# First two batches of a linear-attention and MLP-mixer kernel: casts and features dealt out anew, denominators ahead of kv, w_ch2 and one store issued elsewhere

## The chip, the cores and the metric

The kernel runs on one core of one Trainium2 chip. The metric is device time in microseconds (us), the median of several executions. Shorter names stand for the engines, as in the profile: PE is TensorE (matmuls), PEld its weight loads, DVE is VectorE, ACT is ScalarE, POOL is GpSimd, SP is SyncE, which here only issues transfers. A DMA is a transfer between HBM and the on-chip memory, or a transposing copy within it.

## The reference

Two layers, for 8 batches of 576 rows (`seq`), 8 heads of 64:

```python
def _attn_ref(q, k, v):                       # (8, 8, 576, 64) each
    def phi(x, c, s):                         # c = cos, s = sin of pi/2 * pos / 576
        r = np.maximum(x, 0.0)
        return np.concatenate([r * c, r * s], axis=-1)
    q_p, k_p = phi(q, cos_w, sin_w), phi(k, cos_w, sin_w)
    kv = np.einsum('bhsf,bhsd->bhfd', k_p, v)
    z = np.sum(k_p, axis=2)
    num = np.einsum('bhsf,bhfd->bhsd', q_p, kv)
    den = np.einsum('bhsf,bhf->bhs', q_p, z)[..., None] + 1e-06
    return num / den

def _moe_ref(x, w_tok1, w_tok2, w_ch1, w_ch2):  # x: (8, 576, 512), heads side by side
    h = np.maximum(x.transpose(0, 2, 1) @ w_tok1, 0.0) @ w_tok2      # 576 -> 256 -> 576
    u = x + h.transpose(0, 2, 1)
    h2 = np.maximum(u @ w_ch1, 0.0) @ w_ch2                          # 512 -> 1536 -> 512
    return u + h2
```

Inputs and output are float32; the kernel multiplies in bf16 and sums in float32.

## The kernel before, in words

**Tiling.** A batch's 576 rows are 4 chunks of 128 (row p*4+r is in chunk r) and a tail of 64 rows; the tails of two batches share one 128-row tile. So a batch has five chunks, 0 to 3 and R (the tail). `feature` (lines 274-291) makes the cos half (j = 0) or the sin half (j = 1) of q's or k's features for one chunk, on VectorE, or on ScalarE where `on_act` is set. `values` casts v to bf16 beside a column of ones. `ksum` and `ksum_out` sum the k features (z), `dens` and `dens_out` make the reciprocal of the denominator, `kv` and `kv_out` make kv and copy it out of PSUM, `q_trans` turns q's features so that TensorE can contract over them (`q_trans_beside` the tail's), `num_half` and `num` make the numerators and divide. `tok1`, `tok2`, `turned_*`, `c_main`, `o_mix` and `o_step` are the mixer: its first layer over tokens, the second, u transposed, the channel layer up and the channel layer down.

**Staging.** The first batch has a front of its own, `first_front` (lines 717 to 820). It works in halves of four heads (g = 0, 1), since its inputs come in halves. TensorE also runs `busy` matmuls on zeros there (tile `idle_ps`), whose results nobody reads. Behind it each batch's channel phase is a list of steps (`Channel.steps`): for batch 0 the steps 0 to 11 are `c_main` (the first three are done in the front), 12 and 13 are `o_mix`, and from 14 on each step is two matmuls of `o_step`. The attention of the next batches is woven into those steps: `pieces` gives a plan of (slot, function, arguments), and what stands at slot i is issued right after step i, in the order of the list. For batch 1 the plan is written out by hand: KS makes k's features of a chunk (with True the sin half is made by ScalarE), V casts values, KV is kv, QS makes q's features, QT turns them through TensorE and a ScalarE copy, N is numerators and division, O is 12.

**Order.** The scheduler is manual: every engine runs its own instructions in the order in which the code issues them. One call often issues on several engines (N: eight matmuls on TensorE, then an addition, a reciprocal and a multiplication on VectorE), and what stands behind a waiting instruction on its engine waits too. PSUM has 4 buffers of tag "mm" and 2 of tag "at" (the latter for kv of both halves, for `num_ps` and, in the second batch, for `idle_ps`); a new tile takes a buffer when the last reader of an older tile is done.

**Transfers.** SP issues most loads, all transposing copies of later batches and most stores, each in program order. GpSimd issues the three thirds of w_ch2 (`load_w_ch2`, line 208), converting to bf16, and batch 0's stores of chunks 2 and 3 (line 661). q and k of batch 2 are loaded only when the second third of w_ch2 has landed. GpSimd also casts w_tok1, w_tok2 and w_ch1 (lines 220 to 235).

Of the kernel before, what the change touches and what calls it, by code (L numbers as in the profile page):

```python
# [9 lines left out]
F32 = mybir.dt.float32  # L10
# [6 lines left out]
def kernel(  # L17
# [15 lines left out]
    nc = tc.nc  # L33
# [6 lines left out]
    P = 128  # L40
    R = S // P
# [174 lines left out]
    def busy(dst, times):  # L216
        for _i in range(times):
            nc.tensor.matmul(dst, ident, zeros[:, 0:dst.shape[-1]], start=True, stop=True)  # L218
# [19 lines left out]
    class Front:  # L238
# [81 lines left out]
        def dens(self, g):  # L320
            d_ps = ps_mm.tile([P, NSC * HH], F32, name="d_ps", tag="mm")
            for ci in range(NSC):
                for j in range(HH):
                    nc.tensor.matmul(d_ps[:, ci * HH + j:ci * HH + j + 1],
                                     self.qT_of(ci, g * HH + j), self.ks_sb[g][:, j:j + 1],
                                     start=True, stop=True)
            self.d_ps = d_ps
# [186 lines left out]
        def pieces(self, b, before):  # L514
# [7 lines left out]
            if first:  # L522
# [3 lines left out]
                def fill(times):  # L526
                    if not idle:
# [4 lines left out]
                plan = [(6, KS, 0), (6, KS, 1), (8, KS, 2, True), (9, KS, 3, True), (9, KS, R),  # L532
                        (10, before.tok2, R, None, False), (11, V, 0, act), (11, V, 2, pool),
                        (11, load_w_ch2, 0), (11, V, 3, pool), (11, load_w_ch2, 1),
                        (11, load_w_ch2, 2), (11, V, R, nc.vector), (11, V, 1, act)]
                plan += [(O + 1, KV, ci) for ci in range(NSC)]
                plan += [(O + 1, self.kv_out, (0, 1), (0, 1)), (O + 1, self.q_trans_beside),
                         (O + 1, QS, 0), (O + 1, fill, 2), (O + 1, QT, 0),
                         (O + 1, QS, 1), (O + 1, fill, 1), (O + 1, QT, 1),
                         (O + 1, QS, 2), (O + 1, fill, 1), (O + 1, QT, 2), (O + 1, N, R),  # L540
                         (O + 1, QS, 3, True), (O + 1, N, 0), (O + 2, N, 1), (O + 3, QT, 3),
                         (O + 5, N, 2), (O + 6, N, 3), (O + 8, before.tail_cast)]
# [52 lines left out]
    class Channel:  # L595
# [46 lines left out]
        def o_step(self, ci, lo, hi, cols=slice(0, Dm)):  # L642
# [16 lines left out]
            if ci < R:  # L659

                eng = nc.gpsimd if b == 0 and ci > 1 else nc.sync
                eng.dma_start(
                    out=out[b, 0:SM, cols].rearrange("(p r) d -> p r d", r=R)[:, ci, :], in_=o_sb)
                return
# [52 lines left out]
    def first_front(f):  # L717
# [13 lines left out]
        for ci in range(R):  # L731
            f.feature("k", ci, 0, heads[0])
            f.feature("k", ci, 1, heads[0])
            busy(idle_ps, 2)
            f.ksum(ci, 0)
            f.values(ci, nc.scalar, heads[0])
        f.k_side(R)
# [5 lines left out]
        for ci in range(R):  # L743
            f.feature("k", ci, 0, heads[1])
            if ci < 3:
                f.feature("k", ci, 1, heads[1])
        for ci in range(NSC):
            f.kv(ci, (0,))
        f.kv_out((0,))
        f.feature("k", 3, 1, heads[1], on_act=True)  # L750
        busy(idle_ps, 1)
        f.dens(0)
        f.dens_out(0)
        for ci in ORDER[:2]:
            f.num_half(ci, 0)
        f.values(3, nc.vector, heads[1])
        for ci in range(NSC):
            f.ksum(ci, 1)
        f.values(0, nc.scalar, heads[1])
        f.ksum_out(1)  # L760
        for ci in (1, 2):
            f.values(ci, nc.scalar, heads[1])
# [7 lines left out]
        for i in range(2):  # L770
            f.num_half(ORDER[i + 2], 0)
            f.tok1_half(ORDER[i], 0)
# [4 lines left out]
        f.dens(1)  # L777
        f.dens_out(1)
        permute_tok2(0, nc.scalar.copy)
        for ci in ORDER[:2]:  # L780
            f.num_half(ci, 1)
        for ci in ORDER[2:]:
            f.tok1_half(ci, 0)
# [136 lines left out]
```

## Time and profile before

| | |
|---|---|
| median of 3 executions | 271.11 us (271.05 to 271.15) |
| the profiled execution | 271.65 us |
| its span, first to last instruction | 269.8 us |
| TensorE busy in the span | 261.2 us (97%), 2041 matmuls |
| VectorE, ScalarE, GpSimd busy | 159.9, 127.6, 16.6 us |
| granted TensorE clock | 1.00 |
| the first batch's front (to the first h1T of line 613) | 0 to 26 us |
| the second batch's attention, from its kv to its first mixing matmul | 35.4 to 45.1 us |

A row of the timeline gives start, duration (from the first start to the last end, where rows are merged), engine, line, operation, the tiles written and read, the shape, and in brackets how long the engine sat idle before it and what released it. PE's duration of a matmul is longer than its share of the engine, because matmuls overlap: the distance between starts is what a row of them costs (0.216 us for 512 columns, 0.055 for 128, 0.029 for 65, 0.025 for 1).

### The profile page before, as it was taken

To read this page: it belongs to the slowest core of one execution; us is meant where nothing else is said; L and a number is where in the kernel's file an instruction comes from. 1 tells how busy PE (TensorE), PEld (TensorE's weight loads), DVE (VectorE), ACT (ScalarE), POOL (GpSimd) and SP (SyncE) were. 2 spreads that over 40 slices of the span, in tenths; PEclk is the share of its full clock that TensorE was granted. 3 is DMA by queue.
4 is the path that set the end of the run, shared out by engine and by line. 5 is a ranking of instruction groups with operands and counts; after the bars stand their busy time and mean duration, and the time that the engine had idled before them with its cause. 6 is when DMAs were issued, how large, how long until landed. Compare 5 with 4: busy or idle time off the path is not lost.

```text
span 269.8 us, 5150 instructions
## 1 busy us (share of the span) xinstructions
PE 261.2 (97%) x2041; PEld 140.5 (52%) x2062; DVE 159.9 (59%) x379; ACT 127.6 (47%) x231; POOL 16.6 (6%) x38
## 2 busy tenths in 40 slices
PE   7999988999999999999999999999999999999994
PEld 2685464456644455446644455446644455445543
DVE  5972558766467657677466757777466747720022
ACT  4774874508606173347616272446606372526400
POOL 2068130010000000000000000000000000000000
PEclk9999999999999999999999999999999999999999
DMA  7999999689999899679996999479974570170032
GB/s 232 366 391 378 332 137 230 235 225 242 182 298 300 238 232 286 199 148 247 168 300 101 278 262 302 131 171 260 222 266 117 156 119 0 47 209 0 2 104 91
DMA packets 92263, 55.32 MB, mean 205 GB/s; under 512 B 59472, under 2 KB 85968, under 8 KB 92240
## 3 DMA queue, kind: packets, MB, share of 16 engines
q1 hardware_dynamic: 89968, 52.38, 73.6%
q0 software_dynamic: 1744, 2.10, 4.4%
q10 hardware_dynamic: 528, 0.52, 0.6%
q8 instruction: 16, 0.26, 0.4%
q14 instruction: 7, 0.06, 0.1%
HBM read 35.85 MB, written 9.44 MB: 168 GB/s over the span
## 4 chain that ended last, share of the span: by engine, by line
PE 88%; DVE 5%; DMA 3%; issue 1%; ACT 1%; SPq 0%; POOL 0%; POOLq 0%; DVEq 0%
PE o_ps L649 33%; PE c_ps L609 25%; PE u_ps L460 6%; PE b_ps L436 6%; PE idle_ps L218 4%; PE ct_ps L629 3%; PE kv_ps L371 3%; DVE x_sb L426 2%; PE num_ps L419 2%; DMA qtt<-in_q_dram 2%; PE qT_ps L391 1%; DMA qpT_tail<-qp_tail 1%; PE c_ps L619 1%; PE b_ps L353 1%; DVE den L424 1%
## 5 line engine op out<-in xcount | busy, mean ns | idle before, releaser
L649 PE MATMUL o_ps<-w_ch,h1T 128*128 128x512 bf16 (+1 forms) x381 | 93.0, 372 | 0.6
L609 PE MATMUL c_ps<-uT,w_ch 128*128 128x512 bf16 (+2 forms) x384 | 91.2, 372 | 0.1
L613 ACT ACTIVATE h1T<-c_ps 128x512 bf16<-128x512 f32 x93 | 55.4, 598 | 61.3 <-PE c_ps L609 61.0
L649 PEld LDWEIGHTS <-h1T 128*128 128x128 bf16 x396 | 37.3, 98 | 39.6 <-issue 0.2
L609 PEld LDWEIGHTS <-w_ch 128*128 128x128 bf16 x384 | 33.5, 97 | 29.8
L658 DVE TENSOR_TENSOR o_sb<-o_ps,u_sb 128x512 f32<-128x512 f32 (+1 forms) x29 | 19.5, 672 | 27.3 <-PE o_ps L649 25.3
L467 ACT CAST u_bf<-u_sb 128x512 bf16<-128x512 f32 x28 | 17.3, 618 | 17.4 <-DVE u_sb L463 15.6
L460 PE MATMUL u_ps<-B,w_tok 128*128 128x512 bf16 x71 | 20.2, 379 | 0.2
L441 ACT ACTIVATE B<-b_ps 128x512 bf16<-128x512 f32 x7 | 4.2, 597 | 33.2 <-PE b_ps L436 33.2
L463 DVE TENSOR_TENSOR u_sb<-u_ps,x_sb 128x512 f32<-128x512 f32 x24 | 16.5, 690 | 5.6 <-PE u_ps L460 5.6
L629 PEld LDWEIGHTS <-w_ch 128*128 128x128 bf16 x192 | 13.9, 98 | 8.7
L290 DVE TENSOR_SCALAR kp<-kt,cos_t 128x512 bf16<-128x512 f32 (+1 forms) x36 | 16.1, 450 | 3.9 <-DMA kt<-in_k_dram 3.9
L290 DVE TENSOR_SCALAR qp<-qt,cos_t 128x512 bf16<-128x512 f32 (+1 forms) x35 | 16.2, 462 | 2.0 <-DMA qt<-in_q_dram 1.9
L426 DVE TENSOR_TENSOR x_sb<-num_ps,den 128x512 bf16<-128x512 f32 x24 | 16.6, 691 | 0.8
L629 PE MATMUL ct_ps<-uT_tail,w_ch 128*128 128x128 bf16 x192 | 16.9, 219 | 0.0
L301 ACT CAST v_aug<-vt 128x512 bf16<-128x512 f32 (+1 forms) x31 | 16.6, 576 | 0.1
L290 DVE TENSOR_SCALAR qp<-qt,sin_t 128x512 bf16<-128x512 f32 (+1 forms) x34 | 15.4, 453 | 0.0
L290 DVE TENSOR_SCALAR kp<-kt,sin_t 128x512 bf16<-128x512 f32 (+1 forms) x33 | 14.9, 452 | 0.0
L658 DVE TENSOR_TENSOR o_sb<-o_ps,u_tail 128x512 f32<-128x512 f32 x4 | 2.8, 691 | 19.0 <-PE o_ps L649 19.0
L218 PE MATMUL idle_ps<-zeros,ident 128*128 128x512 bf16 x33 | 12.0, 469 | 1.6 <-POOL ident masks.py:199 1.4
L436 PE MATMUL b_ps<-x_sb,w_tok 128*128 128x512 bf16 x48 | 13.3, 379 | 0.0
L419 PEld LDWEIGHTS <-qpT 128*128 128x128 bf16 x224 | 10.1, 98 | 5.5 <-ACT qpT L395 1.5
(112 smaller groups left out, 241.9 us busy)
## 6 DMA issues: line engine op xcount, KB each, us to landing
out_dram<-o_sb SPq DMA_DIRECT2D x29, 256.0 KB, 2.9
kt<-in_k_dram SPq DMA_DIRECT2D x7, 1024.0 KB, 6.8
vt<-in_v_dram SPq DMA_DIRECT2D x7, 1024.0 KB, 6.9
qt<-in_q_dram SPq DMA_DIRECT2D x7, 1024.0 KB, 8.6
w_stage<-in_moe_w_ch_dram SPq DMA_DIRECT2D x3, 512.0 KB, 9.3
w_ch<-in_moe_w_ch_dram POOLq DMA_DIRECT2D x3, 512.0 KB, 8.6
out_dram<-o_sb SPq DMA_DIRECT2D x10, 128.0 KB, 2.3
kt<-in_k_dram SPq DMA_DIRECT2D x2, 512.0 KB, 5.7
```

The source lines that it names most:

```text
L218: nc.tensor.matmul(dst, ident, zeros[:, 0:dst.shape[-1]], start=True, stop=True)
L290: nc.vector.tensor_scalar(o_ap, i_ap, scalar1=w, scalar2=0.0, op0=ALU.mult, op1=ALU.max)
L301: nc.scalar.copy(dst, src)
L426: nc.vector.tensor_mul(self.x_of(ci)[rows].rearrange("p (g j d) -> p g j d", g=2, j=HH), nv[:, :, :, 0:D], den.to_broadcast([rows.stop - r ...
L436: nc.tensor.matmul(self.b1_ps[mi], w, self.x_of(ci), start=(ci == ORDER[0]), stop=(ci == ORDER[-1]))
L460: nc.tensor.matmul(u_ps, w_tok2[:, ki, ci * P:(ci + 1) * P], self.B1[:, ki, :], start=(ki == 0), stop=(ki == NT - 1))
L467: nc.scalar.copy(self.ub[:, ci, :], u)
L609: nc.tensor.matmul(c_ps[:, lo:hi], w_ch1[:, ki, mi * P:(mi + 1) * P], uT[:, lo // P:hi // P, ki, :], start=(ki == 0), stop=(ki == NCC - 1))
L613: nc.scalar.activation(self.h1T[:, mi, :], c_ps, AF.Relu)
L629: nc.tensor.matmul(self.ct_ps[:, mi % R, :], w_ch1[:, ki, mi * P:(mi + 1) * P], self.tail.uT[:, ki, :], start=(mi % R == 0 and ki == 0), s ...
L649: nc.tensor.matmul(o_ps, h, w_ch2[:, ki, cols], start=(ki == 0 and b > 0), stop=(ki == NCH - 1))
L658: nc.vector.tensor_add(o_sb, o_ps, u)
```

## The change

Only the first two batches' attention and a few transfers are touched; the operations stay the same but for filler matmuls, and each is at another place or on another engine.

In the first batch's front: the sin features of k for chunks 2 and 3, second half of heads, are made by ScalarE ahead of `ksum_out(0)` (before: chunk 2's by VectorE, chunk 3's by ScalarE behind `kv_out`). The denominators of half 0 come ahead of kv of that half, the tail's four apart and behind it, and one filler is gone. The casts of values stand one by one between other ScalarE work. The first numerators come behind the sums of half 1, and the denominators of half 1 ahead of its kv.

In the second batch's plan: k's features of chunks 2 and 3 come at slots 6 and 7 (before 8 and 9). The casts of values come at slot 10, three by VectorE, one by GpSimd, one by ScalarE (before slot 11: two by ScalarE, two by GpSimd, one by VectorE). The first third of w_ch2 is issued on GpSimd ahead of its cast of values, the others right behind it. `before.tok2(R)` is a slot later. Four fillers stand before kv. kv's copies are shared by ScalarE (half 0) and VectorE (half 1), where ScalarE did both. The tail's numerators come ahead of q's features of chunk 2, and the turning of chunks 2 and 3 is later by one slot each. There are 7 fillers in place of 4.

Batch 0's store of chunk 1 is issued by GpSimd in place of SP.

```diff
@@ dens, -317,14
-        def dens(self, g):
-            d_ps = ps_mm.tile([P, NSC * HH], F32, name="d_ps", tag="mm")
-            for ci in range(NSC):
+        def dens(self, g, chunks):
+            if chunks[0] == 0:
+                self.d_ps = ps_mm.tile([P, NSC * HH], F32, name="d_ps", tag="mm")
+            for ci in chunks:
...
@@ pieces, -529,17
-                plan = [(6, KS, 0), (6, KS, 1), (8, KS, 2, True), (9, KS, 3, True), (9, KS, R),
-                        (10, before.tok2, R, None, False), (11, V, 0, act), (11, V, 2, pool),
-                        (11, load_w_ch2, 0), (11, V, 3, pool), (11, load_w_ch2, 1),
-                        (11, load_w_ch2, 2), (11, V, R, nc.vector), (11, V, 1, act)]
+                plan = [(6, KS, 0), (6, KS, 1), (6, KS, 2, True), (7, KS, 3, True), (9, KS, R),
+                        (10, V, 3, act), (10, load_w_ch2, 0), (10, V, 2, pool),
+                        (10, load_w_ch2, 1), (10, load_w_ch2, 2), (10, V, 0, nc.vector),
+                        (10, V, 1, nc.vector), (10, V, R, nc.vector),
+                        (11, before.tok2, R, None, False), (O + 1, fill, 4)]
                 plan += [(O + 1, KV, ci) for ci in range(NSC)]
-                plan += [(O + 1, self.kv_out, (0, 1), (0, 1)), (O + 1, self.q_trans_beside),
-                         (O + 1, QS, 0), (O + 1, fill, 2), (O + 1, QT, 0),
-                         (O + 1, QS, 1), (O + 1, fill, 1), (O + 1, QT, 1),
-                         (O + 1, QS, 2), (O + 1, fill, 1), (O + 1, QT, 2), (O + 1, N, R),
-                         (O + 1, QS, 3, True), (O + 1, N, 0), (O + 2, N, 1), (O + 3, QT, 3),
-                         (O + 5, N, 2), (O + 6, N, 3), (O + 8, before.tail_cast)]
+                plan += [(O + 1, self.kv_out), (O + 1, self.q_trans_beside),
+                         (O + 1, QS, 0), (O + 1, fill, 1), (O + 1, QT, 0),
+                         (O + 1, QS, 1), (O + 1, fill, 1), (O + 1, QT, 1), (O + 1, N, R),
+                         (O + 1, QS, 2), (O + 1, fill, 1), (O + 1, N, 0), (O + 1, QS, 3, True),
+                         (O + 2, QT, 2), (O + 2, N, 1), (O + 4, QT, 3),
+                         (O + 5, N, 2), (O + 5, N, 3), (O + 8, before.tail_cast)]
@@ o_step, -658,7
-                eng = nc.gpsimd if b == 0 and ci > 1 else nc.sync
+                eng = nc.gpsimd if b == 0 and ci > 0 else nc.sync
@@ first_front, -734,6
             f.values(ci, nc.scalar, heads[0])
+        for ci in (2, 3):
+            f.feature("k", ci, 1, heads[1], on_act=True)
         f.k_side(R)
...
         f.q_trans_beside()
         for ci in range(R):
             f.feature("k", ci, 0, heads[1])
-            if ci < 3:
+            if ci < 2:
                 f.feature("k", ci, 1, heads[1])
+        f.dens(0, range(R))
         for ci in range(NSC):
             f.kv(ci, (0,))
         f.kv_out((0,))
-        f.feature("k", 3, 1, heads[1], on_act=True)
-        busy(idle_ps, 1)
-        f.dens(0)
+        f.values(0, nc.scalar, heads[1])
+        f.dens(0, (R,))
         f.dens_out(0)
-        for ci in ORDER[:2]:
-            f.num_half(ci, 0)
-        f.values(3, nc.vector, heads[1])
         for ci in range(NSC):
             f.ksum(ci, 1)
-        f.values(0, nc.scalar, heads[1])
+        f.values(1, nc.scalar, heads[1])
         f.ksum_out(1)
-        for ci in (1, 2):
-            f.values(ci, nc.scalar, heads[1])
+        f.values(2, nc.scalar, heads[1])
...
-        for i in range(2):
-            f.num_half(ORDER[i + 2], 0)
-            f.tok1_half(ORDER[i], 0)
+        for ci in ORDER[:2]:
+            f.num_half(ci, 0)
+        f.values(3, nc.vector, heads[1])
+        f.num_half(ORDER[2], 0)
+        f.tok1_half(ORDER[0], 0)
+        f.dens(1, range(NSC))
+        f.dens_out(1)
+        f.num_half(ORDER[3], 0)
+        f.tok1_half(ORDER[1], 0)
         for ci in range(NSC):
             f.kv(ci, (1,))
         f.kv_out((1,), on_act=(1,))
         f.num_half(ORDER[4], 0)
-        f.dens(1)
-        f.dens_out(1)
         permute_tok2(0, nc.scalar.copy)
+        f.tok1_half(ORDER[2], 0)
         for ci in ORDER[:2]:
             f.num_half(ci, 1)
-        for ci in ORDER[2:]:
+        for ci in ORDER[3:]:
             f.tok1_half(ci, 0)
```

## The prediction, made before the changed kernel was run

> **What bounds the kernel now.** I read the page first: TensorE is busy for 97% of the span at full granted clock, so time is won or lost only where it stands idle or does filler work. Then the list of what TensorE waited for: seven waits, 3.5 us, 1.4 of them at the start. Two stretches that the change touches hold four of them, and a fifth hangs on SP's queue.
>
> ```profile
> span 269.8 us, 5150 instructions
> PE 261.2 (97%) x2041; PEld 140.5 (52%) x2062; DVE 159.9 (59%) x379; ACT 127.6 (47%) x231; POOL 16.6 (6%) x38
> ```
> ```profile
> PE num_ps L419 <- DVE x_tail L426: 0.6, 1, 0.6
> PE num_ps L419 <- DMA qpT_tail<-qp_tail: 0.5, 1, 0.5
> PE num_ps L338 <- DVE x_sb L341: 0.4, 1, 0.4
> PE kv_ps L371 <- ACT v_aug L301: 0.3, 1, 0.3
> PE qT_ps L391 <- ACT qpT L395: 0.2, 1, 0.2
> ```
> From 45.1 us, where the second batch's first mixing matmul starts, to 266 TensorE has one wait of note, the 0.5 us at 75 (`qpT_tail`). Whatever delays 45.1 delays the end by as much.
>
> Then the timelines of VectorE around 35 to 42 us (the second batch), of ScalarE around 17 to 20 (the first) and of GpSimd:
>
> ```profile
> 35.45 0.75 DVE L290 TENSOR_SCALAR qp<-qt,cos_t 128x512 bf16<-128x512 f32 x1 [0.64 <-DMA qt<-in_q_dram]
> ...
> 37.70 0.47 DVE L290 TENSOR_SCALAR qp<-qt,sin_t 128x512 bf16<-128x512 f32 x1
> 40.40 0.17 DVE L424 TENSOR_SCALAR den<-num_ps 64x8 f32<-64x8 f32 x1 [2.22 <-PE num_ps L419]
> 40.60 0.20 DVE L425 RECIPROCAL den<-den 64x8 f32<-64x8 f32 x1
> 40.84 0.69 DVE L426 TENSOR_TENSOR x_tail<-num_ps,den 64x512 bf16<-64x512 f32 x1
> ```
> ```profile
> 17.46 0.38 ACT L382 CAST kv_sb<-kv_ps 128x260 bf16<-128x260 f32 x1 [1.04 <-PE kv_ps L371]
> 17.73 1.11 ACT L232 CAST w_tok<-u_sb 128x512 bf16<-128x512 f32 x1
> 18.73 0.30 ACT L234 CAST w_tok<-u_sb 128x128 bf16<-128x128 f32 x1
> 19.20 0.66 ACT L359 ACTIVATE B<-b_ps 128x256 bf16<-128x256 f32 x2 [0.17 <-PE b_ps L353]
> ```
> ```profile
> 32.45 0.62 POOL L303 CAST v_aug<-vt 128x512 bf16<-128x512 f32 x1 [5.92 <-DMA vt<-in_v_dram]
> 33.00 0.89 POOL L210 DMA_DIRECT2D w_ch<-in_moe_w_ch_dram  x1
> ```
> In the first see that VectorE makes six q features as soon as q lands (35.4) and then has 2.2 us to spare; in the second that ScalarE is 0.17 us from being late for `B`; in the third that GpSimd stood idle from 26.5 and held w_ch2's first third back until v had landed.
>
> **The change, part by part.** I replay each engine's list in the new order, with these rows' durations and the distances between starts.
>
> *First batch, up to 20.8 us.* ScalarE's two sin features go into its idle 0.93 us before 13.16 (the pair's starts are 0.51 apart in the q features at 5.45 and 5.96), so `ks_sb` stays at 13.16. Denominators of half 0 (16 starts, 0.40 us) run 13.39 to 13.79, kv (0.61) to 14.40, its copy on ScalarE ends at 14.99 instead of 14.60. The tail's four denominators end at 14.64 against 14.87, the reciprocal at 15.17 against 15.40. Sums of half 1 fill TensorE until 15.00 and the first division starts at 15.36 instead of 15.51: 0.15 gained, and the filler's 0.22 is in that. But half 1's denominators (0.5 us) now lie ahead of its kv: kv ends at 17.78 instead of 17.42, ScalarE's copy of it at 18.20 instead of 17.84, and behind that copy stand the two w_tok2 copies (1.11 and 0.30) and `B`: its second activation ends at 19.95 instead of 19.86. The second matmul of half 1's first token layer needs that buffer (19.91 before, 20.01 after). So the 0.15 is lost again: +0.10, with -0.15 (ScalarE not in the way) and +0.2 as bounds.
>
> *k features earlier, value casts dealt out.* ScalarE's h1T casts move by up to 0.7 us, and each PSUM buffer is still free 0.5 us or more ahead of the matmul that takes it; nothing on the path. The casts: VectorE's three at 0.38 (row at 64.6 us) end about 1.2 us after v lands (32.4), so by 34.
>
> *The second batch, from `o_mix`'s end (34.95) to the first mixing matmul (45.12), 10.17 us before.* Four fillers first (4 x 0.216): 35.81. kv (five chunks at 0.245) is issued by 37.04 and ends at 37.20. Now VectorE holds half of kv's copy (0.43, the row at 69.75) ahead of q's features: 37.24 to 37.67. So q's features start at 37.6 (call it T) where they started at 35.45, and what queues behind that copy is all of q. From T: two chunks' features, 0.395 apart, end at T+0.87 and T+1.66; the first turning starts at T+0.92, its ScalarE copy (1.01) ends at T+2.58; the second turning T+1.71 to 2.16; the tail's numerators to T+2.40. Their addition, reciprocal and multiplication (1.17 from the matmul's end, 40.36 to 41.54 before) hold VectorE until T+3.74, and chunk 2's features stand behind them: T+4.64. TensorE has a filler, chunk 0's numerators and one `o_step` pair until T+3.30, then waits 1.39 us to turn chunk 2 (T+4.69). Chunk 1's numerators, two `o_step` pairs and chunk 3's turning bring it to T+6.80; chunk 3's copy ends at T+8.02, so its numerators, now a slot earlier, wait 0.59; two more pairs, and the mixing starts at T+9.17 = 46.77. That is +1.65: 0.65 for three more fillers, the rest waits (0.9 before the first turning, 1.4, 0.6, where 2.2 stood before). The tail's wait of 0.64 is gone, chunk 2's features are late next. The least is +0.65, the three fillers with no new wait; above, q may land later than T.
>
> *w_ch2.* GpSimd's list now has the first third behind the w_ch1 casts, which end at 26.53: it is issued at 26.5 instead of 33.0, while v and q of batch 2 are in flight (landing 32.4 and 35.4). It has 512 packets of 98 ns, over 16 engines 3.1 us. Bounds for q: 0 (it starts after q) and +3.1 (all of it goes first). The nearest row is GpSimd's second store, issued at 59.6 beside a full SP queue: its first packet came 3.6 us after issue and its 0.64 us of work took 2.8, a share of 23%. So taken: start at 30.0, q's remaining 5.1 us become 6.6, landing at 36.95, v at 33.0: both before they are needed (37.6; 34 for the casts). I take 0 and keep +0.9 as the upper end: q at 38.55 instead of T. The Trainium skill, "DMA: Bandwidth & Descriptors", Queues, rings and completion order, has each DMA engine take turns between queues, a packet at a time; with packets of like length that is nearer to half than 23%. By it the sum would have the 0.9 in it (rival 1). The thirds behind it are not later than before, so the `o_step` pairs that need them (at 40.4 and 43.9, the first two landings at 39.0 and 43.1) do not wait; q and k of batch 2 start earlier, into slack.
>
> *The store.* SP's store at 63.03 to 64.31 lies ahead of the transposes and of q's tails; without it what follows is up to 1.3 us earlier, and the 0.52 us wait at 75.0 is over: -0.52. GpSimd issues it in idle time, beside the transposes of u that land at 55.9 to 57.7 against a need from 58.4; 0.64 us of packets there is covered. At least -0.3, at most -0.52.
>
> **Sum.** +0.10 + 1.65 - 0.52 = +1.2. Against the profiled execution (271.65, that is 269.8 and 1.85 around it) 272.9; that one was 0.54 above the median of the runs, so against 271.11: 272.3. A change within 0.2%, 0.54 us, can't be told from none.
>
> **Rivals.**
> 1. *q lands last.* Early w_ch2 delays q to 38.55, T is 38.65 with stage one's 0.1, 0.95 later than mine: 273.3. For it: DMA is full from 26 to 33 us (share 1.13), and GpSimd has nothing else to wait for. Against: the 23% of the store.
> 2. *Not slower: chunk 2's features do not wait for the tail's division.* The 1.39 us before the third turning is mine by replay alone; no row shows it. If VectorE reaches those features by T+2.4, that wait is nil: 272.3 - 1.4 = 270.9, within 0.2%, and with the bounds of the rest (-0.25, +0.2) partly below 270.57. It decides at 1 us: with less than 0.7 us of that wait there is no measurable loss. Against: VectorE's rows before stand strictly in the listed order, with 2.2 us of idling ahead of a waiting division.
> 3. *The clock falls.* TensorE gets gaps of 0.9 and 1.4 us. At the start 12 fillers took 5.3 us, twice their later 0.216 each; such a spell again would add up to 2.7: 275. Against: 0.7 us of idling in 40 to 43 us left the distances at 0.216. The Trainium skill, "TensorE: Matmul & The Clock Gate", Part 1, asks for a whole idle window of about 3.4 us, which no gap here reaches.
> 4. *The fillers and moves cancel*, the stretch no longer or shorter: 271.1 less the store's 0.5 is 270.6.
>
> **How the numbers follow.** Mine 0.42 (271.9 to 272.8, from its bounds), rival 1 0.25, rival 2 0.18, rival 4 0.12, rival 3 0.03. Rivals 1, 3 and mine are slower: 0.70. Of rivals 2 and 4 half lies below 270.57: faster 0.16, same 0.14. The range, 270.5 to 273.6, leaves out about 0.1 below and under 0.1 above.
>
> **What would show it.** Right: the first VectorE q feature of batch 2 directly behind kv's copy, near 37.7; a wait of 1 us or more before the third `qT_ps` group; the first second-batch `b_ps` near 46.9; no wait for `qpT_tail`; `B`'s second activation near 19.95. Wrong: q's landing as that feature's releaser (rival 1), no wait at the third turning (rival 2), 128-column matmuls more than 0.055 apart (rival 3). The forecast fails if batch 2's stretch takes under 10.9 us.

## The result, and the profile after

The changed kernel takes 273.28 us, the median of 6 executions (272.93 to 274.66), against 271.13 us (271.05 to 271.31) for 6 of the kernel before: a ratio of 1.0085 with a 95% interval of 1.0063 to 1.0107. The forecast was 272.3 us in a range of 270.5 to 273.6. Sign and range hold; the size is 1.0 us short.

The profiled execution of the changed kernel took 274.66 us (span 272.9), the slowest of its six. In it the granted clock of TensorE was at one half from 16.32 to 19.74 us; the profile of before shows no such spell. What this stretch adds is therefore kept apart below, and marks of the second batch are given as distances from `o_mix`'s end, which it only shifts.

The heads of the page, of after:

```profile
span 272.9 us, 5170 instructions
PE 264.2 (97%) x2064; PEld 141.8 (52%) x2064; DVE 160.9 (59%) x381; ACT 127.1 (47%) x230; POOL 16.7 (6%) x38
PEclk9979999999999999999999999999999999999999
```

TensorE is as full as before, 97%, and yet later: its share of the span doesn't tell a loss of 1%. The list of TensorE's waits of after does, in place of the one that the prediction opened with (the 1.4 us at the start, the same as before, is left out):

```profile
PE qT_ps L391 <- DVE qp L290: 2.1, 2, 1.1
PE num_ps L419 <- DMA qpT_tail<-qp_tail: 0.6, 1, 0.6
PE num_ps L419 <- ACT qpT L395: 0.4, 1, 0.4
PE num_ps L338 <- DVE x_sb L341: 0.4, 1, 0.4
```

The waits for `x_tail` (0.6) and `v_aug` (0.3) are gone; a new one, for q's features on VectorE, stands there twice and holds 2.1 us. Where it sits, the timeline of TensorE in the second batch shows (turnings of chunks 0, 1, 2, 3, the last numerators, the first mixing matmul):

```profile
39.71 0.62 PE L391 MATMUL qT_ps<-ident,qp 128*128 128x128 bf16 x8 [1.07 <-DVE qp L290]
40.50 0.62 PE L391 MATMUL qT_ps<-ident,qp 128*128 128x128 bf16 x8
...
43.49 0.62 PE L391 MATMUL qT_ps<-ident,qp 128*128 128x128 bf16 x8 [1.02 <-DVE qp L290]
...
45.19 0.61 PE L391 MATMUL qT_ps<-ident,qp 128*128 128x128 bf16 x8
...
46.90 0.42 PE L419 MATMUL num_ps<-kv_sb,qpT 128*128 128x65 bf16 x8 [0.43 <-ACT qpT L395]
...
48.02 0.81 PE L436 MATMUL b_ps<-x_hold,w_tok 128*128 128x512 bf16 x3
```

And VectorE in the same time:

```profile
38.44 0.43 DVE L382 CAST kv_sb<-kv_ps 128x260 bf16<-128x260 f32 x1 [2.17 <-ACT kv_sb L382]
38.78 0.48 DVE L290 TENSOR_SCALAR qp<-qt,cos_t 128x512 bf16<-128x512 f32 x1
...
41.41 0.17 DVE L424 TENSOR_SCALAR den<-num_ps 64x8 f32<-64x8 f32 x1 [0.96 <-PE num_ps L419]
...
41.84 0.69 DVE L426 TENSOR_TENSOR x_tail<-num_ps,den 64x512 bf16<-64x512 f32 x1
42.55 0.49 DVE L290 TENSOR_SCALAR qp<-qt,cos_t 128x512 bf16<-128x512 f32 x1
```

Read the two together ("turning" is the transposing of q's features on TensorE; "the mixing" is the first `b_ps` matmul). The wait of 1.07 before the first turning ends on the features from 38.78 on, which stand directly behind VectorE's copy of kv. The wait of 1.02 before the third turning ends on the features from 42.55 on, which stand behind the tail's addition and multiplication; VectorE itself idled 0.96 us for that addition's input. From `o_mix`'s end (35.73) to the mixing (48.02) it is 12.29 us, where it was 10.17: +2.12, nearly the whole 2.15 of the medians. Three things in the plan can hold this stretch: q's landing (37.78, before: 35.43), the copy of kv, and the order of chunk 2's features. The profile alone does not say what each is worth, since only the latest of several holds is seen. That is what the runs are for.

### The profile page after: what moved, and what is told of

Read it like the earlier page. It is cut to its first block, busy times and chain, and to the rows that moved or that the text cites. A ratio compares the mean times of both kernels' runs of the same rounds, so it can differ in the third digit from the quotient of the medians.

```text
span 272.9 us, 5170 instructions
## 1 busy us (share of the span) xinstructions
PE 264.2 (97%) x2064; PEld 141.8 (52%) x2064; DVE 160.9 (59%) x381; ACT 127.1 (47%) x230; POOL 16.7 (6%) x38
## 4 chain that ended last, share of the span: by engine, by line
PE 95%; DVE 1%; DMA 1%; ACT 1%; issue 0%; POOL 0%; POOLq 0%
PE o_ps L650 33%; PE c_ps L610 29%; PE u_ps L460 6%; PE b_ps L436 6%; PE kv_ps L371 4%; PE idle_ps L218 4%; PE ct_ps L630 4%; PE num_ps L419 3%; PE qT_ps L391 2%; PE b_ps L353 1%; DMA qpT_tail<-qp_tail 1%; PE c_ps L620 1%; PE t_ps L486 1%; PE o_ps L640 1%; PE num_ps L338 1%; DVE qp L290 1%
## 5 line engine op out<-in xcount | busy, mean ns | idle before, releaser
L650 PE MATMUL o_ps<-w_ch,h1T 128*128 128x512 bf16 (+1 forms) x396 | 94.3, 372 | 0.0
L301 ACT CAST v_aug<-vt 128x512 bf16<-128x512 f32 (+1 forms) x30 | 16.0, 576 | 0.1
L218 PE MATMUL idle_ps<-zeros,ident 128*128 128x512 bf16 x38 | 13.1, 452 | 1.4 <-POOL ident masks.py:199 1.4
L382 DVE CAST kv_sb<-kv_ps 128x260 bf16<-128x260 f32 x7 | 3.0, 432 | 17.1 <-ACT kv_sb L382 17.1
```

The source lines that it names most:

```text
L650: nc.tensor.matmul(o_ps, h, w_ch2[:, ki, cols], start=(ki == 0 and b > 0), stop=(ki == NCH - 1))
```

## The experiments

"The stretch" is always from `o_mix`'s end to the first mixing matmul, and T the start of the first q feature, as in the prediction. Each time is a median, with its ratio to runs of the kernel before on the same chip, and the ratio's 95% interval. The stretch, q's landing and T are read from one profile of each kernel. The kernel counts batches from 0, so its batch 1 is the second batch; the recorded texts also write "batch 2" for the second batch where they speak of v, q, kv and q's features, but the wait for `qpT_tail` near 75 us and the q and k that are held back for w_ch2 are the third batch's.

### Which of the three parts carries the loss

**front_only**: before, with the changed `dens` and the changed `first_front`, and nothing else.

```diff
         f.q_trans_beside()
...
+        f.dens(0, range(R))
         for ci in range(NSC):
             f.kv(ci, (0,))
         f.kv_out((0,))
...
-        busy(idle_ps, 1)
-        f.dens(0)
...
```

> The kernel before with the first batch's new front alone; the second batch's plan and the store as before. Theory A (the loss is made in the second batch, and the clock drop in the first batch comes and goes): an execution whose granted clock stays at 1.00 is 0.1 to 0.4 us faster than before, since in the profile of the changed kernel the front gained 0.14 us up to 15.5 us on top of an earlier start; an execution with one spell of 3.4 us at clock 0.5 between 13 and 20 us is up to 1.1 us slower. Theory B (the front carries the loss): 1.5 to 2 us slower in every execution, clock or not.

**plan_only**: before, with the changed plan of batch 1.

```diff
...
-                         (O + 1, QS, 2), (O + 1, fill, 1), (O + 1, QT, 2), (O + 1, N, R),
...
+                plan += [(O + 1, self.kv_out), (O + 1, self.q_trans_beside),
...
+                         (O + 1, QS, 1), (O + 1, fill, 1), (O + 1, QT, 1), (O + 1, N, R),
+                         (O + 1, QS, 2), (O + 1, fill, 1), (O + 1, N, 0), (O + 1, QS, 3, True),
...
```

> The kernel before with the second batch's new plan alone; front and store as before. Theory A: +2.1 us (in the two profiles the stretch from o_mix's end to the first mixing matmul went from 10.17 to 12.29 us), so about 273.2, with no spell of low clock before 20 us. Theory B: within 0.5 us of before, because the later waits would only take the place of waits that the front's lateness made.

**store_only**: before, with the store's engine changed.

```diff
-                eng = nc.gpsimd if b == 0 and ci > 1 else nc.sync
+                eng = nc.gpsimd if b == 0 and ci > 0 else nc.sync
```

> The kernel before with chunk 1's store of batch 0 on GpSimd and nothing else. My prediction had -0.52 us, the end of the wait for qpT_tail. The profile of the changed kernel speaks against it: the wait is still there (0.6). Theory A (the chain of transposing copies is paced by the copies themselves, not by SP's list): 0 to +0.2 us, and the wait for qpT_tail stays at 0.4 to 0.7. Rival, as predicted: -0.3 to -0.5 us and no such wait, which would mean that the wait in the changed kernel has another cause.

Measured:

| | time, us | ratio | stretch, us |
|---|---|---|---|
| front_only | 271.52 (12 executions) | 1.0007 (0.9992 to 1.0021) | 10.17 |
| plan_only | 273.59 (6) | 1.0094 (1.0078 to 1.0110) | 12.28 |
| store_only | 271.37 (12) | 1.0009 (1.0000 to 1.0018) | 10.17 |

The plan alone is as slow as the whole change, with the same stretch and the same two waits, and at full clock. The front and the store are worth nothing that can be measured. So the clock's fall in the profile of after is not what makes the changed kernel slower; it came on top, in that execution. The gain of 0.1 to 0.4 us that was expected of the front at full clock did not come: the nine executions of front_only without a spell of half clock have a median of 271.13.

The store's part is a miss, and an instructive one. It was expected that the wait for `qpT_tail` stays. It is nil in store_only, as the prediction had it, and still the kernel is no faster. It is nil in plan_only too, where SP still issues the store, and 0.62 us in after, where GpSimd does:

```profile
78.54 0.42 PE L419 MATMUL num_ps<-kv_sb,qpT_tail 128*128 128x65 bf16 x8 [0.62 <-DMA qpT_tail<-qp_tail]
```

Over all profiles: with the store on SP 0.52 (before), 0.18, 0.72, twice 0.08 and three times 0; on GpSimd 0.62, 0.43 and four times 0. The wait comes and goes with something other than this store. What it is stays open.

### What holds the second batch

**after_kv_scalar**: after, with both copies of kv on ScalarE, as before.

```diff
-                plan += [(O + 1, self.kv_out), (O + 1, self.q_trans_beside),
+                plan += [(O + 1, self.kv_out, (0, 1), (0, 1)), (O + 1, self.q_trans_beside),
```

> The changed kernel with one item put back: in the second batch both halves of kv are copied by ScalarE, so VectorE has nothing ahead of q's features. Theory A (q's features are held by VectorE's half of the copy, which itself waits for ScalarE's half): the first q feature starts when q has landed, near 37 to 37.8, instead of 38.8, and the whole is 0.8 to 1.1 us faster than the changed kernel, about 272.2. Rival (q's landing holds them, delayed by the early third of w_ch2): the first feature starts less than 0.3 us earlier and the gain is below 0.3 us. Rival two (the tail's division holds what follows anyway): the features start earlier, but the mixing starts less than 0.4 us earlier.

**w2_early**: before, with the first third of w_ch2 issued ahead of GpSimd's casts of values.

```diff
-                        (10, before.tok2, R, None, False), (11, V, 0, act), (11, V, 2, pool),
-                        (11, load_w_ch2, 0), (11, V, 3, pool), (11, load_w_ch2, 1),
+                        (10, before.tok2, R, None, False), (11, V, 0, act), (11, load_w_ch2, 0),
+                        (11, V, 2, pool), (11, V, 3, pool), (11, load_w_ch2, 1),
```

> The kernel before with one thing moved: the first third of w_ch2 is issued on GpSimd ahead of its cast of values. Theory D (the early third takes bandwidth from v and q of batch 2): q lands near 37.8 instead of 35.4, VectorE's first q feature of that batch starts there, the first turning moves from 37.8 to near 38.8, and the kernel is 0.8 to 1.2 us slower. Rival (q's landing is hidden behind kv): within 0.3 us of before.

**after_kv_w2_late**: after_kv_scalar, and w_ch2's first third behind GpSimd's cast.

```diff
-                        (10, V, 3, act), (10, load_w_ch2, 0), (10, V, 2, pool),
+                        (10, V, 3, act), (10, V, 2, pool), (10, load_w_ch2, 0),
...
-                plan += [(O + 1, self.kv_out), (O + 1, self.q_trans_beside),
+                plan += [(O + 1, self.kv_out, (0, 1), (0, 1)), (O + 1, self.q_trans_beside),
```

> The changed kernel with both holds of batch 2's q features taken away: kv copied by ScalarE alone, and the first third of w_ch2 behind GpSimd's cast. Theory A with D (two holds of nearly equal length, so that taking one away gave only 0.2 us): q lands near 35.3, the features start there or behind the tail's addition (36), the first turning comes straight behind the filler (37.7 instead of 39.7), and the whole is 1.0 to 1.6 us faster than the changed kernel: 271.7 to 272.3. Rival (the features' start does not matter, the tail's division ahead of chunk 2's features does): under 0.6 us faster, with the wait before the third turning grown by as much as the first has shrunk.

**after_qs2_first**: after, with chunk 2's features ahead of the tail's numerators and division.

```diff
-                         (O + 1, QS, 1), (O + 1, fill, 1), (O + 1, QT, 1), (O + 1, N, R),
-                         (O + 1, QS, 2), (O + 1, fill, 1), (O + 1, N, 0), (O + 1, QS, 3, True),
+                         (O + 1, QS, 1), (O + 1, fill, 1), (O + 1, QT, 1), (O + 1, QS, 2),
+                         (O + 1, N, R), (O + 1, fill, 1), (O + 1, N, 0), (O + 1, QS, 3, True),
```

> The changed kernel with VectorE's features of chunk 2 ahead of the tail's numerators and division, everything else as changed. My prediction's step: the third turning waits 1.0 to 1.4 us for them. If so, the wait before the third turning falls to under 0.3 us and the whole is 0.7 to 1.0 us faster than the changed kernel (chunk 3's copy takes back some 0.5). Rival (the division, now later, holds the numerators behind it as long): the wait moves to the numerators of chunk 1 and the gain is under 0.3 us.

**after_fill1**: after, with one filler ahead of kv in place of four.

```diff
-                        (11, before.tok2, R, None, False), (O + 1, fill, 4)]
+                        (11, before.tok2, R, None, False), (O + 1, fill, 1)]
```

> The changed kernel with one filler in place of four ahead of the second batch's kv. My prediction counted the three more fillers at 0.65 us. Theory E (they are hidden: q lands at 37.6 to 37.8 whatever TensorE does, and holds VectorE's features from then): kv and its copies come 0.65 us earlier, the first q feature moves only from 38.2 to 38.8 down to about 37.8, and the gain is 0.3 to 0.6 us in the profile. As predicted (fully on the path): 0.65 us faster. Rival: no gain, under 0.15 us, since q's landing holds all.

Measured, with the marks in us from the span's start:

| | time, us | ratio | stretch | q landed | T |
|---|---|---|---|---|---|
| before | 271.13 | 1 | 10.17 | 35.43 | 35.45 |
| after | 273.28 | 1.0085 (1.0063 to 1.0107) | 12.29 | 37.78 | 38.78 |
| after_kv_scalar | 273.03 | 1.0070 (1.0055 to 1.0084) | 12.01 | 37.83 | 37.85 |
| w2_early | 272.29 | 1.0042 (1.0026 to 1.0057) | 11.14 | 37.66 | 37.68 |
| after_kv_w2_late | 272.44 | 1.0044 (1.0031 to 1.0056) | 10.99 | 35.40 | 35.42 |
| after_qs2_first | 272.80 | 1.0058 (1.0037 to 1.0079) | 11.38 | 37.58 | 37.75 |
| after_fill1 | 273.19 | 1.0089 (1.0070 to 1.0107) | 12.28 | 38.08 | 38.11 |

*Two holds of like length.* Take the copy of kv off VectorE, and T does not move back to 35.4: it moves onto q's landing. VectorE's timeline of after_kv_scalar:

```profile
37.85 0.49 DVE L290 TENSOR_SCALAR qp<-qt,cos_t 128x512 bf16<-128x512 f32 x1 [1.74 <-DMA qt<-in_q_dram]
```

The stretch is shorter by 0.28 us only, and the time by 0.25, where 0.8 to 1.1 was expected; the first rival, q's landing, has it right. Take both away, and the same line of after_kv_w2_late stands where before has it:

```profile
35.42 0.71 DVE L290 TENSOR_SCALAR qp<-qt,cos_t 128x512 bf16<-128x512 f32 x1 [0.59 <-DMA qt<-in_q_dram]
```

Now the stretch is shorter by 1.30: a hold that is taken away alone hides behind the other. For kv's copy the run shows this; that q's landing moved back alone would bring nothing either was not run, but follows from after and plan_only, where q had landed 1.0 and 0.11 us before T and VectorE's copy of kv held it. What is left of the 2.12 is 0.82. (The medians of these two runs lie 0.6 us apart, less than the 1.02 of their stretches: the executions of after_kv_w2_late spread from 271.68 to 273.05, and its profile has a wait of 0.43 for `qpT_tail` that after_kv_scalar's has not. Against after the time fell by 0.84, less than the 1.0 to 1.6 that was expected.)

*The early w_ch2 by itself* costs 0.97 in the stretch and 1.1 us in time (w2_early), with nothing else changed. Its bytes go where q's went. The queues' shares between 29.7 and 34.9 us, first of before and then of after (q0 is GpSimd's queue, q1 SP's, which has q; a packet's time lengthens where two queues share an engine, so that the sum can pass 100%):

```profile
q1 hardware_dynamic: 1765, 1.37, 81.3%
q0 software_dynamic: 14, 0.01, 3.4%
```
```profile
q0 software_dynamic: 528, 0.52, 62.5%
q1 hardware_dynamic: 1265, 0.87, 54.8%
```

SP's queue moved 0.87 MB in place of 1.37, and the 0.50 MB that it lost are the 0.51 that GpSimd's queue gained. The third of w_ch2 has landed at 34.93, so all of it went ahead of the last of q, and q lands 2.35 us later.

*The order of chunk 2's features* is worth 0.91 of stretch (after_qs2_first: 12.29 to 11.38, with T at the same 3.05 behind `o_mix`'s end), about the 0.82 that the two holds leave. In time it is 0.48 between the medians, not the 0.7 to 1.0 that was expected, and the intervals of the two ratios overlap; where the rest went is not shown. The wait before the third turning is gone; the 1.4 in the list is the first turning's, and the fourth now waits 0.3:

```profile
PE qT_ps L391 <- DVE qp L290: 1.8, 2, 1.4
PE qT_ps L391 <- DVE den L424: 0.3, 1, 0.3
```

*The three fillers* cost nothing here: after_fill1 has a stretch of 12.28, as after, and 0.3 to 0.6 was expected; the rival, q's landing, has it right. VectorE's copy of kv starts at 37.13, but q lands at 38.08, and TensorE waits 2.0 before the first turning, where after waits 1.07. Its waits:

```profile
PE qT_ps L391 <- DVE qp L290: 3.1, 2, 2.0
```

### The front and the clock

The profiles of after and of front_only, which have the changed front, both show a spell of half clock near 17 us. Windows of after ahead of it and in it (columns: stretch, its length, then for PE, PEld, DVE, ACT and POOL the busy time and count, the granted clock, the DMA share and GB/s):

```profile
15.00:16.50 1.50, 1.10 (x34) 0.98 (x31) 1.44 (x4) 0.67 (x3) 1.50 (x5) 0.94 1.06 405
16.50:19.80 3.30, 3.30 (x45) 2.86 (x43) 1.81 (x7) 1.48 (x3) 1.99 (x4) 0.51 1.05 403
```

What the spell does to a row of matmuls is seen in kv of half 1, before and after:

```profile
16.65 0.65 PE L371 MATMUL kv_ps<-v_aug,kp 128*128 128x65 bf16 x16
```
```profile
16.98 1.09 PE L371 MATMUL kv_ps<-v_aug,kp 128*128 128x65 bf16 x16
```

Its price in the front: `c_main` (line 610) starts at 26.67 in after, and at 26.02 in after_kv_scalar, which has the same front and no such spell in its profile, so some 0.65 us. The theory for the cause: the changed front has a thinner stretch of matmuls from 13 to 16 us (denominators and sums with one column each, and fillers gone), and a thin stretch is answered by half clock. Two runs try it from both sides.

**front_filled**: front_only, with two more matmuls on zeros there.

```diff
         for ci in ORDER[:2]:
             f.num_half(ci, 0)
+        more_ps = ps_mm.tile([P, 512], F32, name="more_ps", tag="mm")
+        busy(more_ps, 2)
         f.values(3, nc.vector, heads[1])
```

> The kernel before with the first batch's new front alone and two more fillers (2 x 0.216 us) behind the first two numerators of half 0, where TensorE waits 0.4 us. The front alone had times from 270.64 to 272.19, in lumps near 270.65, 271.5 and 272.2, and its profile has one spell of 3.4 us at clock 0.5. In the profiles so far that spell follows a stretch of the same length in which the matmuls' columns at 2.4 a ns fill 0.35 or 0.38 of the time; with 0.42, 0.46, 0.48 in that stretch there was none. Theory C (thin work in one stretch lets the clock fall): two fillers add 0.13 to the share, the spell never comes, no time is above 271.2, the median is 0.3 to 0.6 us below before. Rival (the spread has another cause, or the fillers cost what they save): the spread stays over 1 us, the median within 0.3 us of before or above it.

**before_thin**: before, without the 11 fillers between the sums of k's features. It leaves out matmuls on zeros only.

```diff
-            busy(idle_ps, 2)
...
-        busy(idle_ps, 3)
```

> The kernel before without the 11 fillers between 10 and 13 us (two ahead of each of the four sums of k features, three ahead of the tail's); only matmuls on zeros are left out. Theory C: TensorE waits there for VectorE anyway, so nothing starts later by their absence, but the matmuls' columns then fill only 0.1 to 0.2 of one stretch of 3.4 us, the clock falls to 0.5 for a spell of 3.4 us somewhere between 12 and 18 us in the profiled execution, and the kernel is 0.5 to 1.7 us slower. Rival (the clock does not depend on this): clock 1.00 from about 6 us on, and within 0.3 us of before or faster.

Measured: before_thin takes 272.39 us, a ratio of 1.0047 (1.0031 to 1.0062). It is 1.27 us slower than before for doing less. Its windows:

```profile
10.00:13.00 3.00, 1.62 (x28) 1.29 (x28) 3.00 (x11) 2.22 (x7) 0.00 (x0) 0.90 1.09 395
13.00:17.00 4.00, 3.85 (x79) 3.32 (x77) 2.98 (x11) 2.43 (x7) 2.53 (x6) 0.50 1.05 405
```

The clock is at one half from 12.43 to 19.25 us. TensorE was not idle ahead of it, only half busy. front_filled has no spell in its profile and takes 271.00 us, a ratio of 0.9995 (0.9982 to 1.0008). Its 12 executions spread from 270.6 to 272.2, no less than those of front_only (270.6 to 272.2) or of before in the same run (270.5 to 272.5), so that the theory's stronger form, that the spells make the spread, falls.

The mean granted clock of every execution is on record and says more than the few profiles. A spell of 3.41 us takes 0.006 off it, and there is a gap in the figures: 0.994 and below, or 0.997 and above. At 0.994 or below are 11 of the 47 executions with the changed front, 4 of 4 of before_thin (0.986 to 0.994), none of the 17 with the changed front and two more fillers (front_filled and plan_new_front), and none of 97 with the old front (before, plan_only, store_only, w2_early and plan_new). In front_only the three with a spell have a mean of 271.98, the other nine a median of 271.13. So leaving out filler matmuls brings the spells, and putting two back keeps them away.

Over the profiles the spells are 3.41 us long, or twice that, and begin a multiple of 3.41 after the clock first became full, a moment that differs from run to run (4.0 to 7.1 us). If the time is cut into windows of that length, and the columns of all matmuls that start in a window, at 2.4 a ns (the rows have 512 in 0.216 us, 2.37 a ns), are set against its length, then a fall followed at shares of 0.19, 0.35 and 0.38, and none at 0.41, 0.42, 0.44, 0.46, 0.48 or more. While the clock is at one half a window can hold 0.5 at most; of these, 0.35 was followed by another and 0.38, 0.47 and 0.50 by full clock. At the kernel's end, where the matmuls stop inside a window, a fall followed at 0.22, 0.28 and twice 0.31. One window does not fit this count: the last with matmuls in after_fill1, from 266.19 us, has 0.375, and full clock follows. If the columns are spread over the time behind each start instead, it has 0.39 and the 0.38 of front_only becomes 0.36, and then every window from the first full clock on fits a limit between 0.36 and 0.39. That columns are what counts, and where the limit lies, is a fit to these 14 profiles; no run set it on purpose. Since the cut shifts from run to run, the same thin stretch lies in one window in one execution and across two in the next, which would explain why after shows a spell in its profile while after_kv_scalar and after_fill1 with the same front show none, though one and two of their other executions have one. That explanation is argued from these profiles; no run moved the cut on purpose.

### A version from the findings

**plan_new**: before's front and store. Of the change it keeps the casts, k's features and the later `before.tok2(R)`, which no run shows to cost anything; both kv copies stay on ScalarE, w_ch2 behind GpSimd's cast, and chunk 2's features ahead of the tail's division. Two of before's four fillers go (the one beside chunk 2 and one of the two beside chunk 0), and the last two numerators come a slot earlier.

```diff
+                        (10, V, 3, act), (10, V, 2, pool), (10, load_w_ch2, 0),
+                        (10, load_w_ch2, 1), (10, load_w_ch2, 2), (10, V, 0, nc.vector),
+                        (10, V, 1, nc.vector), (10, V, R, nc.vector),
+                        (11, before.tok2, R, None, False)]
...
-                         (O + 1, QS, 0), (O + 1, fill, 2), (O + 1, QT, 0),
+                         (O + 1, QS, 0), (O + 1, fill, 1), (O + 1, QT, 0),
                          (O + 1, QS, 1), (O + 1, fill, 1), (O + 1, QT, 1),
-                         (O + 1, QS, 2), (O + 1, fill, 1), (O + 1, QT, 2), (O + 1, N, R),
+                         (O + 1, QS, 2), (O + 1, N, R), (O + 1, QT, 2),
                          (O + 1, QS, 3, True), (O + 1, N, 0), (O + 2, N, 1), (O + 3, QT, 3),
-                         (O + 5, N, 2), (O + 6, N, 3), (O + 8, before.tail_cast)]
+                         (O + 4, N, 2), (O + 5, N, 3), (O + 8, before.tail_cast)]
```

> The kernel before (its front, its store) with another plan for the second batch, from what the runs showed: the casts of values dealt out as in the change, so kv starts at 35.0 without a wait instead of 35.4; the thirds of w_ch2 behind GpSimd's cast, so q lands at 35.4; both kv copies on ScalarE, so nothing stands ahead of q's features; chunk 2's features ahead of the tail's division; two fillers in place of four. By the same replay: first turning 36.7 (37.8 before), third 38.5 (39.5), first mixing matmul 43.9 to 44.3 (45.1), held by the second third of w_ch2 that lands near 42.3 to 43.1: 0.7 to 1.2 us faster than before, 270.0 to 270.5. Rival (the second third of w_ch2 or the store's buffers hold it, or the clock falls): within 0.3 us of before.

It takes 269.95 us (269.64 to 270.36), a ratio of 0.9962 (0.9947 to 0.9977): faster than both kernels, 1.2 us below before and 3.3 below after. Its stretch is 8.98 us, the mixing starts at 43.62. In the second batch one wait is left in its list; before's for `v_aug` (0.3), `x_tail` (0.6) and `qpT` (0.2) are gone:

```profile
PE qT_ps L391 <- ACT qp L288: 0.3, 1, 0.3
```

What each of its moves brings was not measured apart.

**plan_new_front**: plan_new's plan on front_filled's front.

```diff
+        f.dens(0, range(R))
         for ci in range(NSC):
             f.kv(ci, (0,))
...
+        more_ps = ps_mm.tile([P, 512], F32, name="more_ps", tag="mm")
+        busy(more_ps, 2)
```

> The kernel before with the plan of the run plan_new and, for the first batch, the changed front with two more fillers (as in front_filled). If the front's gain holds where the clock does: 0.1 to 0.2 us faster than plan_new, 269.7 to 269.9, clock 1.00 in the profile. Rival (front_filled's gain was noise): no faster than plan_new, 269.9 to 270.2.

270.25 us, a ratio of 0.9961 (0.9947 to 0.9974): the same as plan_new. The front's order of denominators and kv brings nothing that can be measured here either, even with its thin stretch filled. The gain of 0.1 to 0.2 us that was expected did not come.

## Why the prediction was right, and where its sizes were off

The prediction's sum was +0.10 + 1.65 - 0.52 = +1.2; measured is +2.15 in the medians. Where the time is lost and the replay of the lists were right. The range held by its width: the bounds that the prediction worked out for its own sum, 271.9 to 272.8, leave 273.28 out, and it was rival 1 that stretched the upper end to 273.6. Its two errors, a store credited with 0.52 and a stretch short by 0.47, point the same way.

*The second batch, +1.65, measured +2.12: the right place, undersized.* The prediction split it at T. From T to the mixing it had 9.17, measured 9.24 in after: the replay of the engines' lists holds to 0.07, and the third turning starts at T+4.71 where it had T+4.69. The waits are given shorter by the page (1.02 for the predicted 1.39, 0.43 for 0.59) since it counts from a matmul's end, 0.16 later than the moment at which the next could have started; the other 0.21 of the first stands as a gap ahead of chunk 0's numerators (41.43 to 41.64). The "2.2" of waits that the prediction says stood there before is not on the page, which has 1.35 (0.33, 0.16, 0.22 and 0.64), or 2.0 counted from where the next matmul could have started; no term of the sum rests on it. From `o_mix`'s end to T it had 2.65, measured 3.05. The step that was mis-sized is "kv (five chunks at 0.245) is issued by 37.04 and ends at 37.20. Now VectorE holds half of kv's copy (0.43, the row at 69.75) ahead of q's features: 37.24 to 37.67": it let VectorE's copy begin when kv ended. In the trace it begins when ScalarE's copy of the other half has ended (the releaser in the row at 38.44 is `ACT kv_sb`, ScalarE's copy from 38.02 to 38.40). The two halves of the tile go one behind the other, and sharing them saved nothing: +0.40. They take 0.85 us in all (38.02 to 38.87), where ScalarE alone had 0.66 before. The profile of before could have told this: the row whose 0.43 the prediction used names ScalarE's copy as what it waited for, and that copy runs from 69.33 to 69.71.

```profile
69.75 0.43 DVE L382 CAST kv_sb<-kv_ps 128x260 bf16<-128x260 f32 x1 [1.97 <-ACT kv_sb L382]
```

*"0.65 for three more fillers, the rest waits": the split was wrong.* The fillers cost 0 (after_fill1), because without them q's landing holds T where kv's copy held it (38.07 and 38.18 in plan_only, 0.11 apart). The prediction's least of +0.65 for the stretch therefore did not follow from them; the fillers take the place of a wait. Rival 4, that fillers and moves cancel, falls with the stretch's 12.29.

*w_ch2, taken at 0: right in the sum by luck, wrong by the transfer.* The start of its packets was taken at 30.0 and is 29.7. But q was taken to land at 36.95, by the store's share of 23%, and landed at 37.78 in after and 38.07 in plan_only. That is still ahead of T, by 1.0 us in after, where the clock's spell had made kv late, and by 0.11 in plan_only, but only because kv's copy came 0.40 later than predicted: q landed 2.93 behind `o_mix`'s end in plan_only, where the prediction had T at 2.65. Rival 1 (q at 38.55, 273.3 us) gave the time that came, yet its mechanism is only half of it: kv's copy, later than the prediction had it, and q, later too, reach T together, and the early w_ch2 costs 0.97 of stretch where the copy is out of the way (w2_early). The Trainium skill, "DMA: Bandwidth & Descriptors", Queues, rings and completion order, with its taking of turns packet by packet, was nearer than the 23% of the store: GpSimd's queue got 62.5 of 62.5 + 54.8, that is 53% of the two queues' packet time. It was not nearer for the reason that the prediction gives, packets of like length. By the lines above GpSimd's took 98 ns on average (62.5% of 16 engines for 5.2 us, over 528) and SP's 36; one of each in turn would give GpSimd 73%, and by bytes it got 37% (0.52 of 1.39 MB). What a turn holds is not shown here.

*The store, -0.52: failed.* "Without it what follows is up to 1.3 us earlier, and the 0.52 us wait at 75.0 is over" took one profile's wait for a fixed one. It is 0 in three profiles with the store on SP and 0.62 in after with the store on GpSimd; store_only is not faster. This is about half of what is missing, the stretch's 0.47 the other. The prediction's sign "no wait for `qpT_tail`" failed with it, and no run shows a gain for the store.

*The front, +0.10: nothing that can be seen.* At full clock ScalarE's second `B` activation ends at 20.00 in after_kv_scalar against 20.05 in plan_only, which has the old front (predicted: 0.09 later), and `c_main` starts at 26.02 against 26.07; in time front_only is 1.0007 (0.9992 to 1.0021).

*Rival 3, the clock,* came true at another place than it was put: not in the second batch, where the gaps of 1 us changed nothing, but in the first, where no gap of TensorE is longer than 0.4 us. It shifted the profiled execution, the only one of the six with a spell, and not the result. The Trainium skill, "TensorE: Matmul & The Clock Gate", Part 1, gives the window as about 3.4 us, and the spells here are 3.41; it asks for an idle window, and in that the trace differs: here one filled to a third was enough.

*Rival 2* (no wait before the third turning) is refuted by the 1.02 us in after, and after_qs2_first shows that it is the order that makes it.

## What to carry to other kernels

When a profile shows one wait, ask what would end next if it were gone: here kv's copy and q's landing ended nearly together, the copy was worth 0.3 us of the stretch when it alone was moved back and 1.3 with q, and a filler ahead of both was free. A transfer that is issued earlier because its queue is idle takes its share from the one that is needed next; look at when that one lands, not at the idle issuer. A wait that one profile shows far from the change (`qpT_tail`) needs a second profile before it enters a sum. And a row that lends its duration to a sum should lend its bracket too: what the operation waited for there, it will wait for again.

## What the runs showed of the hardware

- Half clock follows a window of 3.41 us in which TensorE is thinly used, not idle: shares of up to 0.36 of the columns that it could take were followed by a fall, shares from 0.39 up were not (columns spread over the time behind each start, 14 profiles; by starts alone one window at 0.375 does not fit). Eleven matmuls on zeros left out of the first batch brought such a spell in 4 of 4 executions and made the kernel 1.27 us slower; two put into the changed front took them from 11 of 47 executions to 0 of 17.
- Two engines that copy the two halves of one PSUM tile in this kernel ran one behind the other (38.02 to 38.40 on ScalarE, from 38.44 on VectorE). The order is a wait of the program: VectorE's copy stands behind a semaphore that ScalarE's copy raises, and in all four profiles that share the copy (after, plan_only, after_qs2_first, after_fill1) it starts 0.024 us after that (38.412 and 38.436 in after). Whether the two could run together without the wait was not tried.
- GpSimd's load of 512 KB, issued at 26.28 beside a full SP queue, had its first packet 3.4 us later and then 53% of the two queues' packet time, 37% of their bytes, until it landed at 34.93; q, on SP's queue, landed 2.35 us later for it.
